# phi_q times KV in a linear-attention kernel: from whole-array matmuls to pairs on two 64-row halves

## The chip, the cores and the metric

The kernel runs on one core of one Trainium2 chip. Its time is the device time of one launch in microseconds (us). The kernel before takes 290.5 us, the median of 4 runs (290.08 to 291.49). A core has a matrix engine (PE, with weight loads shown as PEld), a vector engine (DVE), a scalar engine (ACT), a general engine (POOL), and SP, whose queue issues most DMAs here. PE multiplies a stationary operand, loaded first, with a moving one that streams past it column by column; results go to PSUM, from where DVE or ACT copy them to SBUF. An operand's row in the array is its partition, and both may occupy only a part of the 128 rows.

## The reference

The input x has 2048 rows of 640 features, in bfloat16. One pre-norm transformer block is computed, with linear attention of 32 heads of 20 features, and a gated feed-forward part of width 1536:

```python
qkv = layernorm(x) @ wqkv                       # q, k, v: 32 heads of 20
pq, pk = q @ w_phi, k @ w_phi                   # per head
phi_q = concat(softmax(pq), softmax(-pq))       # 40 features a head
phi_k = concat(softmax(pk), softmax(-pk))
kv, z = phi_k.T @ v, sum(phi_k)                 # per head, over all rows
o = (phi_q @ kv) / (phi_q @ z + 1e-6)
h = x + o @ wo
out = h + (gelu(layernorm(h) @ w_gate) * (layernorm(h) @ w_up)) @ w_down
```

## The kernel before

The 2048 rows are cut into 16 tiles of 128, and four tiles make a block. Matmuls and SP's DMAs run in the order in which the code is written out by hand; a function `weave` puts the steps of the attention of later tiles between the units (`gate_up`, `down`) of the feed-forward part of a block. All engines keep the order of the code, so one that waits holds what stands behind it.

*First stage.* For each tile, x is normalised and transposed. `fold` (L188) multiplies the weights of k, and later those of q, with w_phi, so that the exponent's argument comes out of one product; ACT and DVE in turn copy the result out of PSUM (L208, L210). `k_tile` computes it for k, and ACT makes `E`, exp of plus and of minus the argument. `k_norm` divides on the v side: DVE sums each head's exponentials, and `vt` is v with a column of ones, scaled by the reciprocal, by POOL or DVE (L269). `kv_tile` (L274) accumulates E.T @ vt over all tiles in one PSUM tile `kvp`. It does so for 64 features at a time, in two column halves of the array: features of the first half of a 128-feature chunk go to partitions 0 to 63 of the output, the others to 64 to 127, and each piece takes the four heads that its 64 features can touch, 4 x 21 = 84 columns. There are 20 such matmuls for a tile, two signs by five chunks by two halves.

*KV.* `kv_mask` (L285) writes the heads' own blocks from `kvp` into `KV`, which has 128 features by 5 chunks by 2 signs by 8 heads by 22 columns (20 of v, one of sums, and one of ones, put there beforehand from a mask `hmask`, L354 to L356, by POOL). It takes four instructions on DVE for one sign and four on POOL for the other, because the position of the four heads among the eight of a chunk differs by chunk and half. Products with features of another head are zeroed by the mask.

*Queries.* `q_mm` and `q_exp` make `Eq`, exp of plus and minus the argument of q, features on partitions, in chunks of 128. `attn_a` (L393) multiplies it with KV for one tile of rows: the stationary operand is 128 features of `Eq` by 128 rows, the moving one is the part of `KV` of the heads concerned. The result for all heads and signs, `AB`, has 2 x 32 x 22 columns. They are made in three groups of 11, 11 and 10 heads, the first two in one PSUM tile of two banks, the third in another. A chunk of 128 features touches 7 or 8 heads and may lie in two groups, so there are 14 matmuls for a tile, of 44 to 176 columns:

```python
pieces = [(s, c, max(h0, H0[c]), min(h1, H0[c] + NH[c])) for s in range(2) for c in range(NC)]
pieces = [x for x in pieces if x[2] < x[3]]
```

The first PSUM tile is copied to SBUF by ACT (L412), the second by ACT, and for tiles 0 and 1 by DVE (L415). Steps `attn_b` to `attn_b3` form the denominators (`pr`, `den`, `rd`, `w`) and the output `o` on POOL and DVE; then `o` is transposed, multiplied with wo (`attn_c`, L464), and added to x; the second layernorm follows, and `gate_up` (L504) and `down` (L519).

PSUM tiles of the second half of the program come from a ring of four (`psG2`), each of two banks, in the order of the code: a new tile waits until the one four places earlier has been copied out.

Of the kernel before, what the change touches and what calls it, by code (L numbers as in the profile page):

```python
# [8 lines left out]
BF16 = mybir.dt.bfloat16  # L9
F32 = mybir.dt.float32  # L10
ALU = mybir.AluOpType
# [6 lines left out]
def kernel(  # L18
# [12 lines left out]
    nc = tc.nc  # L31
    P = 128
    S = 2048
    D = 640
    H = 32
    Dh = 20
# [3 lines left out]
    NC = D // P  # L40
    NF = FF // P
    EPS = 1e-5
    HD = D // 2

    H0 = [(P * c) // Dh for c in range(NC)]
    NH = [(P * c + P - 1) // Dh - H0[c] + 1 for c in range(NC)]
# [2 lines left out]
    QT = (15, 15, 15, 15)  # L49
    VC = Dh + 1  # L50
    KC = Dh + 2
    UH = 11
    NU = 3

    G0 = [64 * j // Dh for j in range(2 * NC)]

    x_v = A_x.rearrange("b (p t) d -> p (b t) d", t=NT)
    o_v = out.rearrange("b (p t) d -> p (b t) d", t=NT)
# [3 lines left out]
    const = ctx.enter_context(tc.tile_pool(name="const", bufs=1))  # L62
# [9 lines left out]
    Wo = const.tile([P, NC, D], BF16, name="Wo")  # L72
    Wg = const.tile([P, NC, FF], BF16, name="Wg")
    Wu = const.tile([P, NC, FF], BF16, name="Wu")
    KV = const.tile([P, NC, 2, 8, KC], BF16, name="KV")

    Eq = [const.tile([P, 2, 2, 512], BF16, name=f"Eq{j}") for j in range(NB * NC // 2)]
    ident = const.tile([P, P], BF16, name="ident")
    hmask = const.tile([P, NC, 8], BF16, name="hmask")
    BD = const.tile([P, NC, 8, Dh], BF16, name="BD")  # L80
    nhalf = const.tile([P, 2], F32, name="nhalf")

    def eq(t, c, s):
        j = t // 4 * NC + c
        return Eq[j // 2][:, j % 2, s, t % 4 * P:(t % 4 + 1) * P]
# [4 lines left out]
    def gtile(name):  # L90
        return psG.tile([P, 2, 512], F32, name=name, tag="G")
# [45 lines left out]
    Wq2 = mid.tile([P, NC, D], BF16, name="Wq2")  # L137
# [3 lines left out]
    Wk2 = p1.tile([P, NC, D], BF16, name="Wk2")  # L141
# [5 lines left out]
    WkT = fp.tile([P, NC, D], BF16, name="WkT")  # L147
    WqT = p1.tile([P, NC, D], BF16, name="WqT")
# [25 lines left out]
    for c in range(NC):  # L174
        off = P * c - Dh * H0[c]
        nc.gpsimd.affine_select(out=hmask[:, c, :], in_=hmask[:, c, :], pattern=[[-Dh, 8]],
                                compare_op=ALU.is_ge, fill=0.0, base=off, channel_multiplier=1)
        nc.gpsimd.affine_select(out=hmask[:, c, :], in_=hmask[:, c, :], pattern=[[Dh, 8]],
                                compare_op=ALU.is_ge, fill=0.0, base=Dh - 1 - off, channel_multiplier=-1)
# [5 lines left out]

    warm(NWARM)

    def fold(WT, W2):  # L188


        runs = []
        for c in range(NC):
            lo, hi = H0[c] * Dh, (H0[c] + NH[c]) * Dh
            for u in range(2):
                a, b = max(lo, u * HD), min(hi, (u + 1) * HD)
                if a < b:
                    runs.append((u, c, a, b))
        runs.sort()
        for d in range(NC):
            wa = gtile("wa")  # L200
            for i, (u, c, a, b) in enumerate(runs):
                nc.tensor.matmul(wa[:, u, a - u * HD:b - u * HD], lhsT=WT[:, c, d * P:(d + 1) * P],
                                 rhs=BD[:, c].rearrange("p a b -> p (a b)")[:, a - H0[c] * Dh:b - H0[c] * Dh],
                                 start=(i == 0 or runs[i - 1][0] != u),
                                 stop=(i + 1 == len(runs) or runs[i + 1][0] != u), skip_group_check=True)
            dst = W2[:, d, :].rearrange("p (u f) -> p u f", u=2)
            if d % 2 == 0:
                nc.scalar.copy(dst, wa[:, :, 0:HD])  # L208
            else:
                nc.vector.tensor_copy(dst, wa[:, :, 0:HD])  # L210

    lnp, Ek, Vt = {}, {}, {}

    def ln_st(*tiles, act=True):
        for t, v in zip(tiles, ln_stats(p1, [x_sb[t // 4][:, t % 4, :] for t in tiles], "1", act)):
            lnp[t] = v
# [8 lines left out]
    def ln_tp(t):  # L225
        transpose_to(LN1T[t // 4][:, :, t % 4 * P:(t % 4 + 1) * P], lnp[t], True)
# [22 lines left out]
    def v_tile(t):  # L249
        v_mm(t)  # L250
        v_ev(t)

    def k_tile(t):
        pk = gtile("pk")
        proj(pk, t, Wk2)
        Ek[t] = ev.tile([P, 2, D], BF16, name="E", bufs=8)
        for s in range(2):
            nc.scalar.activation(Ek[t][:, s, :].rearrange("p (u f) -> p u f", u=2), pk[:, :, 0:HD],  # L258
                                 ACTF.Exp, scale=(1.0 if s == 0 else -1.0))
# [12 lines left out]
    kvp = psK.tile([P, 2, 512], F32, name="kvp")  # L272

    def kv_tile(t):  # L274

        for s in range(2):
            for c in range(NC):
                for u in range(2):
                    g0 = G0[2 * c + u]
                    nc.tensor.matmul(kvp[u * 64:(u + 1) * 64, s, c * 4 * VC:(c + 1) * 4 * VC],  # L280
                                     lhsT=Ek[t][:, s, c * P + u * 64:c * P + (u + 1) * 64],
                                     rhs=Vt[t][:, s, g0:g0 + 4, :],
                                     start=(c == 0 and t == 0), stop=(t == NT - 1), skip_group_check=True)

    def kv_mask():  # L285

        kp = kvp[:, :, 0:NC * 4 * VC].rearrange("p s (h f) -> p s h f", f=VC)

        nc.vector.tensor_scalar_add(kp[:, :, :, Dh], kp[:, :, :, Dh], 0.5e-6)
        nc.scalar.copy(acc.rearrange("p c h f -> p (c h f)"), kvp[:, 0, 0:NC * 4 * VC])  # L290
        for s, eng, src in ((1, nc.vector, kvp[:, 1, 0:NC * 4 * VC].rearrange("p (c h f) -> p c h f", h=4, f=VC)),
                            (0, nc.gpsimd, acc)):
            for u, c0, c1 in ((0, 0, 5), (1, 0, 2), (1, 2, 3), (1, 3, 5)):
                h = G0[2 * c0 + u] - H0[c0]
                r = slice(u * 64, (u + 1) * 64)
                eng.tensor_tensor(KV[r, c0:c1, s, h:h + 4, s:s + VC], src[r, c0:c1],
                                  hmask[r, c0:c1, h:h + 4, None].to_broadcast([64, c1 - c0, 4, VC]), ALU.mult)

    pqs = {}

# [10 lines left out]
    def q_exp(j, signs=(0, 1)):  # L311
        for s in signs:
# [19 lines left out]

    nc.vector.tensor_tensor(BD, wphi[:, :, None, :].to_broadcast([P, NC, 8, Dh]),
                            hmask[:, :, :, None].to_broadcast([P, NC, 8, Dh]), ALU.mult)
# [1 line left out]
    v_tile(2)  # L336
    ln_ap(3, on_pe=True)
    ln_st(4, 5, act=False)
    fold(WkT, Wk2)
    ln_tp(3)  # L340
    fp_cm.__exit__(None, None, None)
    ev_cm = tc.tile_pool(name="ev", bufs=1, side="right", reuse_waits="tile")
# [2 lines left out]
    for t in range(NT):  # L345
        k_tile(t)
        if t == 0:
            ln_ap(4, on_pe=True)
            ln_tp(4)
            ln_ap(5, on_pe=True)  # L350
            ln_st(6, 7)
        if t == 1:
            ln_tp(5)
            nc.gpsimd.memset(KV, 0.0)  # L354
            nc.gpsimd.tensor_copy(KV[:, :, 0, :, KC - 1], hmask)
            nc.gpsimd.tensor_copy(KV[:, :, 1, :, 0], hmask)  # L356
        if t == 12:
            fold(WqT, Wq2)
        if t + 3 < NT:
            v_tile(t + 3)  # L360
        if 6 <= t + 5 < NT:
            ln_ap(t + 5, on_act=True)
        if t % 2 == 1 and t + 7 < NT:
            ln_st(t + 7, t + 8)
        k_norm(t)
        if t % 2 == 1 and t >= 5:
            kv_tile(t - 5)
            kv_tile(t - 4)
        if t == 10:
            nc.sync.dma_start(Wo, wo_v)  # L370
            nc.sync.dma_start(Wu, wu_v)
        for j in range(len(QT)):
            if t == QT[j]:
                q_mm(j)
                q_exp(j)
    q = len(QT)
    for t in range(12, NT):
        kv_tile(t)
# [14 lines left out]
    def attn_a(t, dve=False):  # L393

        b = t // 4
        if b not in LN2T:
            LN2T[b] = p2.tile([P, NC, 512], BF16, name="LN2T", bufs=2)
        AB = p2r.tile([P, 2, H, KC], F32, name="AB", bufs=2)
        for v in range(2):
            ab = gtile("ab")  # L400
            for i in range(2 - v):
                h0 = UH * (2 * v + i)
                h1 = min(h0 + UH, H)
                pieces = [(s, c, max(h0, H0[c]), min(h1, H0[c] + NH[c])) for s in range(2) for c in range(NC)]
                pieces = [x for x in pieces if x[2] < x[3]]
                for j, (s, c, ha, hb) in enumerate(pieces):
                    nc.tensor.matmul(  # L407
                        ab[:, i, s * UH * KC + (ha - h0) * KC:s * UH * KC + (hb - h0) * KC],
                        lhsT=eq(t, c, s), rhs=KV[:, c, s, ha - H0[c]:hb - H0[c], :],
                        start=(j == 0), stop=(j == len(pieces) - 1), skip_group_check=True)  # L410
            if v == 0:
                nc.scalar.copy(AB[:, :, 0:2 * UH, :].rearrange("p s (u h) f -> p u s (h f)", u=2),  # L412
                               ab[:, :, 0:2 * UH * KC].rearrange("p u (s f) -> p u s f", s=2))
            else:
                (nc.vector.tensor_copy if dve else nc.scalar.copy)(  # L415
                    AB[:, :, 2 * UH:H, :].rearrange("p s h f -> p s (h f)"),
                    ab[:, 0, 0:2 * UH * KC].rearrange("p (s f) -> p s f", s=2)[:, :, 0:(H - 2 * UH) * KC])
        st[t] = AB

    def attn_b(t, on_pe=False):  # L420
# [222 lines left out]
```

The softmax here doesn't subtract the row's maximum and nothing guards it: scores larger than these inputs give would overflow.

## Time and profile before

The profile is of one execution, and shows what each engine did and waited for.

| | us |
|---|---|
| median of the runs | 290.5 |
| the profiled execution | 290.86 |
| its span, first to last instruction | 289.2 |
| copy of the first part of AB, ACT, L412 | 0.963 each, 16 times |
| copy of the second part of AB, ACT, L415 | 0.536 each, 14 times |
| copy of the second part of AB, DVE, L415 | 0.612 each, twice |

A row of instructions gives the line, engine, operation, tiles written and read, the shape, and busy time with the mean of one in nanoseconds. For matmuls the end, and so the duration, is modelled, and successive matmuls overlap; the distance between starts is what they cost. Three stages matter: up to about 79 us k, v and KV are made; from 79.4 to 103.1 the queries and the attention of the first tiles; then the feed-forward part, with the attention of later tiles between.

### The profile page before, as it was taken

How to read it: one execution, taken by the hardware profiler on the slowest of the kernel's cores; microseconds unless marked ns; L12 is line 12 of the kernel's file. 1: busy time of each engine (PE TensorE's matmuls, PEld its weight loads, DVE VectorE, ACT ScalarE, POOL GpSimd, SP SyncE). 2: the span in 40 equal slices, each digit the busy share in tenths (PEclk: the TensorE clock that was granted, in tenths of full speed). 3: DMA queues.
4: the chain of work that ended last, by engine and by line, in shares of the span. 5: the costliest groups of instructions: out<-in, count | busy, mean ns of one | idle time of the engine just before them, and what ended most of it. 6: DMA issues, size and time to landing. Idle time of an engine off the chain costs nothing.

```text
span 289.2 us, 5553 instructions
## 1 busy us (share of the span) xinstructions
PE 275.7 (95%) x2218; PEld 177.4 (61%) x2233; DVE 167.7 (58%) x287; ACT 144.1 (50%) x228; POOL 98.8 (34%) x207
## 2 busy tenths in 40 slices
PE   7798899989999899999999999999999999999995
PEld 2475577765555688778875555576555567444473
DVE  6689999988367466675623656532484832323322
ACT  2379778765968866536425445331445441123200
POOL 6228977866320223643421136220124340000000
PEclk9999999999999999999999999999999999999999
DMA  7997413290080011425310112222011322000011
GB/s 207 226 329 242 64 32 70 48 354 32 2 272 2 0 22 27 56 59 71 68 45 25 25 23 46 49 54 82 2 31 21 64 45 83 33 1 0 2 45 45
DMA packets 40970, 21.03 MB, mean 73 GB/s; under 512 B 33136, under 2 KB 39280, under 8 KB 40944
## 3 DMA queue, kind: packets, MB, share of 16 engines
q1 hardware_dynamic: 39856, 19.67, 27.9%
q10 hardware_dynamic: 1088, 1.01, 1.1%
q8 instruction: 17, 0.28, 0.4%
q14 instruction: 9, 0.07, 0.1%
HBM read 10.18 MB, written 2.62 MB: 44 GB/s over the span
## 4 chain that ended last, share of the span: by engine, by line
PE 81%; DVE 6%; DMA 5%; ACT 4%; issue 2%; POOL 1%; SPq 0%; ACTq 0%; DVEq 0%; POOLq 0%
PE gu L504 33%; PE pd L519 18%; PE pq L308 7%; PE po L464 7%; PE pv L235 5%; PE pk L235 5%; PE ab L407 3%; DMA Wv<-in_A_wqkv_dram 3%; DVE sk L264 2%; PE kvp L280 2%; DMA oT<-o 1%; DMA LN1T<-ln 1%; ACT Eq L313 1%; DVE vt L269 1%; ACT E L258 1%
## 5 line engine op out<-in xcount | busy, mean ns | idle before, releaser
L507 ACT ACTIVATE g<-gu 128x512 bf16<-128x512 f32 (+1 forms) x60 | 30.7, 512 | 74.9 <-PE gu L504 69.8
L510 DVE TENSOR_TENSOR GT<-gu,g 128x512 bf16<-128x512 f32 (+1 forms) x60 | 34.5, 581 | 56.7 <-ACT g L507 56.5
L504 PE MATMUL gu<-LN2T,Wg 128*128 128x512 bf16 (+1 forms) x293 | 61.4, 335 | 1.6 <-DVE LN2T L130 0.6
L504 PE MATMUL gu<-LN2T,Wu 128*128 128x512 bf16 (+1 forms) x296 | 61.2, 336 | 0.1
L519 PE MATMUL pd<-Wd,GT 128*128 128x320 bf16 x384 | 53.9, 299 | 0.0
L519 PEld LDWEIGHTS <-GT 128*128 128x128 bf16 x384 | 37.5, 98 | 15.6 <-DVE GT L510 0.9
L504 PEld LDWEIGHTS <-Wu 128*128 128x128 bf16 x300 | 29.3, 98 | 22.6
L504 PEld LDWEIGHTS <-Wg 128*128 128x128 bf16 x300 | 29.0, 98 | 21.3 <-issue 1.5
L235 PEld LDWEIGHTS <-LN1T 128*128 128x128 bf16 x320 | 30.5, 98 | 16.9 <-DMA LN1T<-ln 2.8
L269 POOL TENSOR_TENSOR vt<-vS,rs 128x672 bf16<-128x672 bf16 x22 | 34.5, 1588 | 8.9 <-DVE rs L266 7.3
L525 DVE TENSOR_TENSOR y<-pd,x_sb 128x640 bf16<-128x640 f32 (+1 forms) x17 | 13.3, 784 | 30.7 <-PE pd L519 30.7
L235 PE MATMUL pv<-Wv,LN1T 128*128 128x320 bf16 x160 | 24.2, 299 | 4.0 <-DMA LN1T<-ln 2.2
L464 PE MATMUL po<-Wo,oT 128*128 128x320 bf16 x160 | 24.4, 299 | 0.4 <-DMA oT<-o 0.4
L235 PE MATMUL pk<-Wk,LN1T 128*128 128x320 bf16 x160 | 24.2, 299 | 0.3 <-DVE Wk L210 0.3
L445 DVE TENSOR_TENSOR tt<-AB,w 128x1280 bf16<-128x1280 f32 x16 | 23.8, 1486 | 1.2 <-POOL w L438 0.9
L258 ACT ACTIVATE E<-pk 128x640 bf16<-128x640 f32 x32 | 20.7, 702 | 7.0 <-PE pk L235 6.9
L264 DVE TENSOR_REDUCE sk<-E 128x64 f32<-128x1280 bf16 x16 | 23.2, 1450 | 0.8 <-ACT E L258 0.8
L308 PE MATMUL pq<-LN1T,Wq 128*128 128x512 bf16 x96 | 22.7, 379 | 0.6 <-ACT Eq L313 0.4
L412 ACT COPY AB<-ab 128x968 f32<-128x968 f32 x16 | 15.4, 963 | 14.7 <-PE ab L407 14.5
L313 ACT ACTIVATE Eq<-pq 128x1024 bf16<-128x1024 f32 x20 | 19.4, 1025 | 3.4 <-PE pq L308 3.4
L464 PEld LDWEIGHTS <-oT 128*128 128x128 bf16 x160 | 15.5, 98 | 8.0 <-DMA oT<-o 1.2
L487 POOL TENSOR_SCALAR v<-sm 128x1 f32<-128x1 f32 x14 | 8.4, 599 | 31.4 <-DVE x_sb L478 31.4
(75 smaller groups left out, 277.2 us busy)
## 6 DMA issues: line engine op xcount, KB each, us to landing
out_dram<-y SPq DMA_DIRECT2D x15, 160.0 KB, 1.8
Wg<-in_B_w_gate_dram SPq DMA_DIRECT2D x1, 1920.0 KB, 11.3
Wu<-in_B_w_up_dram SPq DMA_DIRECT2D x1, 1920.0 KB, 9.3
Wd<-in_B_w_down_dram SPq DMA_DIRECT2D x1, 1920.0 KB, 7.8
x_sb<-in_A_x_dram SPq DMA_DIRECT2D x2, 640.0 KB, 5.7
Wv<-in_A_wqkv_dram SPq DMA_DIRECT2D x2, 400.0 KB, 8.4
Wo<-in_A_wo_dram SPq DMA_DIRECT2D x1, 800.0 KB, 4.9
x_sb<-in_A_x_dram ACTq DMA_DIRECT2D x1, 640.0 KB, 8.6
```

The source lines that it names most:

```text
L235: nc.tensor.matmul(ps[:, u, 0:HD], lhsT=lnT(t, c), rhs=W[:, c, u * HD:(u + 1) * HD], start=(c == 0), stop=(c == NC - 1))
L258: nc.scalar.activation(Ek[t][:, s, :].rearrange("p (u f) -> p u f", u=2), pk[:, :, 0:HD], ACTF.Exp, scale=(1.0 if s == 0 else -1.0))
L264: nc.vector.reduce_sum(sk, Ek[t].rearrange("p s (h f) -> p (s h) f", f=Dh), axis=AX.X)
L269: eng.tensor_tensor(vt[:, s], vS[t % 6], rs[:, s * H:(s + 1) * H, None].to_broadcast([P, H, VC]), ALU.mult)
L308: nc.tensor.matmul(pqs[j][:, i, :], lhsT=Wq2[:, kc, c * P:(c + 1) * P], rhs=LN1T[b][:, kc, :], start=(kc == 0), stop=(kc == NC - 1))
L313: nc.scalar.activation(Eq[j][:, :, s, :], pqs[j], ACTF.Exp, scale=(1.0, -1.0)[s])
L445: nc.vector.tensor_tensor(tt.rearrange("p s (h f) -> p s h f", f=Dh), num, w[:, :, :, None].to_broadcast([P, 2, H, Dh]), ALU.mult)
L464: nc.tensor.matmul(po[:, u, 0:HD], lhsT=st[t][:, c, :], rhs=Wo[:, c, u * HD:(u + 1) * HD], start=(c == 0), stop=(c == NC - 1))
L504: nc.tensor.matmul(gu[:, i, 0:n], lhsT=W[:, c, f * P:(f + 1) * P], rhs=LN2T[b][:, c, a0:a1], start=(c == 0), stop=(c == NC - 1))
L507: nc.scalar.activation(g[:, 0:n], gu[:, 0, 0:n], ACTF.Gelu_apprx_tanh)
L510: nc.vector.tensor_tensor(st[b, "g", f][:, a0:a1], gu[:, 1, 0:n], g[:, 0:n], ALU.mult)
L519: nc.tensor.matmul(pd[:, u, 0:HD], lhsT=st[b, "g", f][:, tl * P:(tl + 1) * P], rhs=Wd[:, f, u * HD:(u + 1) * HD], start=(f == 0), stop=(f ...
```

## The change

The features of q are put in another order. In each chunk of 128, the first 64 now belong to heads 0 to 15 and the other 64 to heads 16 to 31; `fold` writes the folded weights of q in that order. For k nothing is reordered, but `kv_tile` takes its 64 features from the first or the second half of the 640, so that the two halves of the partitions of `kvp` hold the same grouping. Every 64 features touch four heads, from head 3c of the half on, whatever the chunk c and the half. So KV has room for 4 heads instead of 8, one mask `kmask` serves all, and `kv_mask` takes one instruction on each engine.

`attn_a` uses 64 rows of the array at a time: a matmul has 64 features and 4 x 22 = 88 columns. Successive matmuls alternate between the upper and the lower rows and write different PSUM tiles, one for heads 0 to 15 and one for heads 16 to 31. There are 20 for a tile, and both PSUM tiles are taken before the first of them. Each is copied out whole, 2 x 352 columns.

```diff
-    KV = const.tile([P, NC, 2, 8, KC], BF16, name="KV")
+    KV = const.tile([P, NC, 2, 4, KC], BF16, name="KV")
...
+    UH = H // 2
+    HALF = (slice(0, 64), slice(64, P))
...
+    kmask = const.tile([P, NC, 4], BF16, name="kmask")
...
-            dst = W2[:, d, :].rearrange("p (u f) -> p u f", u=2)
+            dst, src = W2[:, d, :].rearrange("p (u f) -> p u f", u=2), wa[:, :, 0:HD]
+            if halves:
+                dst = W2[:, d, :].rearrange("p (c u f) -> p u c f", c=NC, u=2)
+                src = src.rearrange("p u (c f) -> p u c f", c=NC)
...
-                    g0 = G0[2 * c + u]
-                    nc.tensor.matmul(kvp[u * 64:(u + 1) * 64, s, c * 4 * VC:(c + 1) * 4 * VC],
-                                     lhsT=Ek[t][:, s, c * P + u * 64:c * P + (u + 1) * 64],
-                                     rhs=Vt[t][:, s, g0:g0 + 4, :],
+                    f0, h0 = u * HD + c * 64, u * UH + 3 * c
+                    nc.tensor.matmul(kvp[HALF[u], s, c * 4 * VC:(c + 1) * 4 * VC],
+                                     lhsT=Ek[t][:, s, f0:f0 + 64], rhs=Vt[t][:, s, h0:h0 + 4, :],
...
-            for u, c0, c1 in ((0, 0, 5), (1, 0, 2), (1, 2, 3), (1, 3, 5)):
-                h = G0[2 * c0 + u] - H0[c0]
-                r = slice(u * 64, (u + 1) * 64)
-                eng.tensor_tensor(KV[r, c0:c1, s, h:h + 4, s:s + VC], src[r, c0:c1],
-                                  hmask[r, c0:c1, h:h + 4, None].to_broadcast([64, c1 - c0, 4, VC]), ALU.mult)
+            eng.tensor_tensor(KV[:, :, s, :, s:s + VC], src, kmask[:, :, :, None].to_broadcast([P, NC, 4, VC]), ALU.mult)
...
-            nc.gpsimd.tensor_copy(KV[:, :, 0, :, KC - 1], hmask)
-            nc.gpsimd.tensor_copy(KV[:, :, 1, :, 0], hmask)
+            nc.gpsimd.memset(kmask, 1.0)
+            for r in HALF:
+                nc.gpsimd.affine_select(out=kmask[r], in_=kmask[r], pattern=[[4, NC], [-Dh, 4]],
+                                        compare_op=ALU.is_ge, fill=0.0, base=0, channel_multiplier=1)
+                nc.gpsimd.affine_select(out=kmask[r], in_=kmask[r], pattern=[[-4, NC], [Dh, 4]],
+                                        compare_op=ALU.is_ge, fill=0.0, base=Dh - 1, channel_multiplier=-1)
+            nc.gpsimd.tensor_copy(KV[:, :, 0, :, KC - 1], kmask)
+            nc.gpsimd.tensor_copy(KV[:, :, 1, :, 0], kmask)
...
-        for v in range(2):
-            ab = gtile("ab")
-            for i in range(2 - v):
-                h0 = UH * (2 * v + i)
-                h1 = min(h0 + UH, H)
...
-                    nc.tensor.matmul(
-                        ab[:, i, s * UH * KC + (ha - h0) * KC:s * UH * KC + (hb - h0) * KC],
-                        lhsT=eq(t, c, s), rhs=KV[:, c, s, ha - H0[c]:hb - H0[c], :],
-                        start=(j == 0), stop=(j == len(pieces) - 1), skip_group_check=True)
...
+        ab = gtile("ab"), gtile("ab")
+        for s in range(2):
+            for c in range(NC):
+                for u, r in enumerate(HALF):
+                    nc.tensor.matmul(ab[u][:, s, 3 * c * KC:(3 * c + 4) * KC], lhsT=eq(t, c, s)[r],
+                                     rhs=KV[r, c, s].rearrange("p h f -> p (h f)"),
+                                     start=(c == 0), stop=(c == NC - 1), skip_group_check=True)
+        for u in range(2):
+            (nc.vector.tensor_copy if dve and u == 1 else nc.scalar.copy)(
+                AB[:, :, u * UH:(u + 1) * UH].rearrange("p s h f -> p s (h f)"), ab[u][:, :, 0:UH * KC])
```

More of the change, by code (lines that the diff above doesn't have):

```diff
@@ L51 @@
     KC = Dh + 2
-    UH = 11
-    NU = 3
-    G0 = [64 * j // Dh for j in range(2 * NC)]
+    UH = H // 2
+    HALF = (slice(0, 64), slice(64, P))
     x_v = A_x.rearrange("b (p t) d -> p (b t) d", t=NT)
@@ L186, with fold @@
     warm(NWARM)
-    def fold(WT, W2):
+    def fold(WT, W2, halves):
         runs = []
@@ L205, in fold @@
                                  stop=(i + 1 == len(runs) or runs[i + 1][0] != u), skip_group_check=True)
-            dst = W2[:, d, :].rearrange("p (u f) -> p u f", u=2)
+            dst, src = W2[:, d, :].rearrange("p (u f) -> p u f", u=2), wa[:, :, 0:HD]
+            if halves:
+                dst = W2[:, d, :].rearrange("p (c u f) -> p u c f", c=NC, u=2)
+                src = src.rearrange("p u (c f) -> p u c f", c=NC)
             if d % 2 == 0:
-                nc.scalar.copy(dst, wa[:, :, 0:HD])
+                nc.scalar.copy(dst, src)
             else:
-                nc.vector.tensor_copy(dst, wa[:, :, 0:HD])
+                nc.vector.tensor_copy(dst, src)
     lnp, Ek, Vt = {}, {}, {}
@@ L338 @@
     ln_st(4, 5, act=False)
-    fold(WkT, Wk2)
+    fold(WkT, Wk2, False)
     ln_tp(3)
@@ L354 @@
             nc.gpsimd.memset(KV, 0.0)
-            nc.gpsimd.tensor_copy(KV[:, :, 0, :, KC - 1], hmask)
-            nc.gpsimd.tensor_copy(KV[:, :, 1, :, 0], hmask)
+            nc.gpsimd.memset(kmask, 1.0)
[6 more added lines that the diff above has]
+            nc.gpsimd.tensor_copy(KV[:, :, 1, :, 0], kmask)
         if t == 12:
-            fold(WqT, Wq2)
+            fold(WqT, Wq2, True)
         if t + 3 < NT:
@@ L398, in attn_a @@
         AB = p2r.tile([P, 2, H, KC], F32, name="AB", bufs=2)
-        for v in range(2):
-            ab = gtile("ab")
-            for i in range(2 - v):
-                h0 = UH * (2 * v + i)
-                h1 = min(h0 + UH, H)
[L404 to L407, printed above, removed]
-                        ab[:, i, s * UH * KC + (ha - h0) * KC:s * UH * KC + (hb - h0) * KC],
-                        lhsT=eq(t, c, s), rhs=KV[:, c, s, ha - H0[c]:hb - H0[c], :],
-                        start=(j == 0), stop=(j == len(pieces) - 1), skip_group_check=True)
[L411 to L417, printed above, removed]
+        ab = gtile("ab"), gtile("ab")
[8 more added lines that the diff above has]
+                AB[:, :, u * UH:(u + 1) * UH].rearrange("p s h f -> p s (h f)"), ab[u][:, :, 0:UH * KC])
         st[t] = AB
```

## The prediction

> **What bounds the kernel now.** The first section of the page and its clock row come first: is one engine the bound, and is it ever slowed?
>
> ```profile
> span 289.2 us, 5553 instructions
> PE 275.7 (95%) x2218; PEld 177.4 (61%) x2233; DVE 167.7 (58%) x287; ACT 144.1 (50%) x228; POOL 98.8 (34%) x207
> PEclk9999999999999999999999999999999999999999
> ```
>
> PE, the matmul engine, is busy for 95% of the span at its full clock, and no other engine reaches 60%. A busy PE need not be a limited one, so next the chain that ended last, summed by line:
>
> ```profile
> PE 81%; DVE 6%; DMA 5%; ACT 4%; issue 2%; POOL 1%; SPq 0%; ACTq 0%; DVEq 0%; POOLq 0%
> PE gu L504 33%; PE pd L519 18%; PE pq L308 7%; PE po L464 7%; PE pv L235 5%; PE pk L235 5%; PE ab L407 3%; DMA Wv<-in_A_wqkv_dram 3%; DVE sk L264 2%; PE kvp L280 2%; DMA oT<-o 1%; DMA LN1T<-ln 1%; ACT Eq L313 1%; DVE vt L269 1%; ACT E L258 1%
> ```
>
> The chain is PE's own instruction stream. The product that the change rewrites, `ab` on L407, holds 3% of it, so this is the most that can be won. The timeline of one call (tile 8), PE and its weight loads:
>
> ```profile
> 151.64 0.83 PEld L407 LDWEIGHTS <-Eq 128*128 128x128 bf16 x14
> 151.78 0.87 PE L407 MATMUL ab<-KV,Eq 128*128 128x154 bf16 x14
> 152.48 1.24 PE L504 MATMUL gu<-LN2T,Wg 128*128 128x512 bf16 x4
> ```
>
> The ends of matmuls are modelled, so I read starts: from 151.78 to 152.48 one call takes 0.70 us of PE, and 16 calls take 11.2. What follows begins at once. Last, the kernel already has one product on two halves of the array: `kvp` on L280, split by columns, in pairs. It is the nearest row to what comes:
>
> ```profile
> 35.23 1.53 PE L235 MATMUL pv<-Wv,LN1T 128*128 128x320 bf16 x10 [1.14 <-DMA LN1T<-ln]
> 36.70 0.95 PE L280 MATMUL kvp<-vt,E 128*64 128x84 bf16 x40
> 37.58 0.85 PE L235 MATMUL pk<-Wk,LN1T 128*128 128x320 bf16 x5
> ```
>
> **Price of a matmul.** Pieces of the chain give start to start: 10 of 512 columns in 2.16 us (216 ns), 10 of 320 in 1.36 (136), 5 of 128 in 0.28 (56). That is 0.417 ns a column plus 2.6 ns each. Check on `ab`: a call has 14 matmuls with 2 x 792 = 1584 columns: 660 + 36 = 696 ns, as measured. So columns, not weight loads, set its time.
>
> **Price of a pair and of the switch.** By this, 84 columns cost 37.6 ns. The ten `pv` that begin at 35.23 have streamed by 36.59, and `pk` begins at 37.58: 0.99 us for the 40 half-array matmuls. As 20 concurrent pairs they need 0.752; one after the other 1.50. They do run in pairs, and 0.235 us are left for entering and leaving. Single rows of the trace place it: 0.093 before the first `kvp`, 0.093 after the last, the rest on slower first pairs and the first full matmul afterwards. The two matmuls of a pair start 2 to 7 ns apart.
>
> **The product, changed.** A call becomes 20 matmuls of 64 rows and 88 columns (39.3 ns), as 10 pairs. The trace has no row-split matmul, so both ends. Low: pairs concurrent, no switch, 0.393 us. High: no overlap and a full switch, 0.786 + 0.235 = 1.02. I take the pair and the switch as `kvp` shows them: 0.393 + 0.235 = 0.63, a gain of 0.07 us a call, 16 x 0.07 = 1.2 us (1.1 to 1.3 by rounding). Most of what the pairing wins (0.31) goes to the switch, because a call is short: ten pairs and out again. Only a pair interval below (0.70 - 0.235) / 10 = 46.5 ns gains at all.
>
> Two rules of the Trainium skill speak against this. "TensorE: Matmul & The Clock Gate", section "Wait — 56ns, not 53.3ns?", gives about 25 ns below which matmul starts never come closer. By it a call is 20 x 25 + 235 = 735 ns, 0.035 over now: +0.6 us in all. The `kvp` row has 40 starts in 0.88 us, 22 ns each with the switch inside, so the floor doesn't hold across two halves, and I go by the row. The same page, section "LDWEIGHTS (loading the stationary operand)", says that a load's time depends on its columns and not on its rows. Then half-height loads are no cheaper, and they rise from 14 to 20 a call. The nearest row: where a 44-column matmul lies between loads of 128 columns, starts are 27 to 28 ns apart, though its columns need 21. If the loads of the two halves cannot overlap, a pair is at least 55 ns and a call 0.55 + 0.235 = 0.785, +1.4 us in all. `kvp` loads 64 columns, not 128, so it cannot exclude this; it stays as a rival.
>
> **What of the gain arrives.** After 103 us PE waits only three times for over 0.1 us (0.42 at 131.4, 0.20 at 142.8, 0.54 at 167.4), so nearly all of it does. Exceptions: from 97.7 to 103.1 the chain runs over ACT (exponentials, two `AB` copies, table load, gelu), and calls 2 and 3 lie beside it: 0.15 lost. I leave about 0.1 for the waits at 131.4 and 167.4, which end on other engines.
>
> **Copies out of PSUM.** Before, 968 elements (963 ns) and 440 (536) on ACT; after, twice 704, by these two points 750 each: 1.50 us as before. The first copy can no longer begin after 10 of 14 matmuls, since both tiles finish together; with the shorter call both are out within 0.1 us of before. For tiles 0 and 1 the second copy is on DVE: 440 elements take 612 ns, and 640 take 823 in the residual add, so 704 take about 890, +0.28. Behind it on DVE are `pr`, `den`, `rd`, `w`, `tt`, `o`, and PE's transpose waits for `o`; at tile 1 it has about 0.4 us to spare, of which two slower copies and an earlier PE take most: 0 to 0.2 lost, I take 0.1. ACT is 0.2 us freer per such tile.
>
> **Buffers.** Both `ab` tiles must now be free at the first matmul; before, the second had 0.48 us more. If PE waits there, the whole queue behind it (gate, up, down) does. Against the evictions of the trace the second had been free for over 0.14 us at each start except call 3 (100.8 us), where it waits 0.1 to 0.3 inside the stretch that ACT bounds. Nothing.
>
> **Edits at zero.** The mask of KV goes from four instructions to one on each engine: DVE 1.35 us to 0.59, POOL 2.16 to 0.89. PE meanwhile runs `pq` up to 81.68; only call 0, 0.75 long instead of 0.70, seems to have waited for POOL, 0.05. POOL's set-up at tile 1: a memset of half the size (1.56 to 0.8), a new memset (0.13), four masks at 0.2, two copies at 0.3: 2.3 us as before. Its cover is POOL's idle time in that stage; without it, 0.1. The regrouping of Wq is in the write of five existing copies, same element count: 0, at most 0.1 each where PE waits on two of them near 60 us. `kvp` keeps number and size of its matmuls. No DMA is added or moved.
>
> **Sum.** -1.2 + 0.15 + 0.1 + 0.1 - 0.05 = -0.9. The profiled execution, 290.86 us around its span of 289.2, would be 289.96; it lay 0.36 above the median of 290.5, and the median becomes 289.6.
>
> **The rivals.**
> - *Loads in turn* (0.17): pairs at 55 ns. For it: 27 ns for a full-width load. Against: halves have rows of their own. +1.4 gives 291.9, a little less if the first load hides in the switch.
> - *Halves in turn* (0.13), the slower side: row halves don't run together as column halves do, for example because both put out to all 128 partitions of PSUM. Place: each of the 160 pairs; price 39.3 ns a pair, 1.02 us a call, +0.32 x 16 = 5.1, 295.6. It decides from the 46.5 ns above. Against it: the two halves write separate banks here.
> - *No switch* (0.14): row halves need no drain, a call is 0.39, -0.31 x 16 = -4.9, of which calls 2 and 3 and DVE's copies keep back 0.9: 286.5. Against it: `kvp` pays it both ways, every time.
>
> **How the numbers follow.** Likeliest (0.55): 289.6, its own range 288.4 to 290.4, for a switch of 0.15 to 0.25 us; the residual 0.01 is anything else. A measurement tells 0.5% from no change, so faster means below 289.05 and slower above 291.95. Faster: 0.37 of the likeliest (0.20) and *no switch*, 0.34. Slower: *halves in turn*, two fifths of *loads in turn*, the residual, 0.21. The rest, 0.45, is the same. The range 286.2 to 292.0 takes in all but *halves in turn* and thin ends.
>
> **What the next profile would show.** Right: `ab` calls start to next start 0.60 to 0.65, pairs 39 ns apart and their halves under 10 ns, 0.09 us of nothing at each end. Starts 27 ns apart mean the loads; 39 apart one by one, the halves in turn; no gap at the ends, no switch. New waits of PE before L408 would break the buffer step; a PE wait over 0.2 us at the transpose of tile 1, the copy step. I am wrong above all if entering row halves costs something else than entering column halves.

## The result and the profile after

The changed kernel takes 289.83 us (median of 29 runs, 288.89 to 292.22) against 290.73 of the kernel before, measured beside it (48 runs): -0.90 us by the medians; the ratio of the runs is put at 0.9973, 95% interval 0.9959 to 0.9986. Forecast was -0.9. The profiled execution took 289.56 us around a span of 287.8, against 290.86 and 289.2.

The engines' shares barely move, from the page of the kernel after:

```profile
span 287.8 us, 5742 instructions
PE 273.9 (95%) x2314; PEld 171.8 (60%) x2329; DVE 167.9 (58%) x284; ACT 143.8 (50%) x228; POOL 98.0 (34%) x209
```

PE is still the bound. It has 96 matmuls and 96 loads more and is busy for 1.8 us less. The same call as in the prediction, tile 8, in the timeline of PE after:

```profile
151.01 0.98 PE L515 MATMUL pd<-Wd,GT 128*128 128x320 bf16 x6
151.92 0.57 PE L408 MATMUL ab<-KV,Eq 64*128 64x88 bf16 x20
152.42 1.04 PE L500 MATMUL gu<-LN2T,Wg 128*128 128x512 bf16 x3
```

Six `pd` at 136 ns from 151.01 have streamed by 151.83, and the next `gu` begins at 152.42: the call costs 0.59 us where it cost 0.70. In it are twenty matmuls, in pairs that run together, and two gaps, 151.83 to 151.92 and one of the same length at the end. Single rows give the starts within this call, in ns from its first:

```
0 3 | 39 42 | 87 90 | 126 129 | 165 168 | 204 207 | 243 247 | 282 286 | 322 325 | 361 364 | next work 498
```

The halves start 3 ns apart and pairs 39, with one step of 48 after the second pair. Sixteen calls, 0.11 each, are 1.8 us. The first whole-array matmul behind a call costs 10 ns more than those after it, so that PE saves 1.6. Not all of that arrives, and PE's waits show where, before and after (us in total, times, longest):

```profile
PE tp L129 <- DVE ln L121: 0.7, 2, 0.4
PE gu L504 <- DVE GT L510: 0.5, 2, 0.3
PE po L464 <- DMA oT<-o: 0.4, 1, 0.4
```

```profile
PE tp L130 <- DVE ln L122: 0.9, 2, 0.6
PE gu L500 <- DVE GT L506: 0.8, 2, 0.5
PE po L460 <- DVE GT L506: 0.5, 1, 0.5
```

The first two waits have grown: PE is earlier and the other engines are not. The `po` rows are two different places. That of before is at 167.4 us and is gone after. That of after is at 142.8 us, where PE needs the transposed `o` and waited 0.20 us before the change. What ended this wait is named differently from trace to trace; by the time of landing it is the DMA of `oT`, as shown further below.

### The profile page after: what moved, and what is told of

Its sections match the earlier page's. It is cut to its first block, busy times and chain, and to the rows that moved or that the text cites. A ratio compares the mean times of both kernels' runs of the same rounds, so it can differ in the third digit from the quotient of the medians.

```text
span 287.8 us, 5742 instructions
## 1 busy us (share of the span) xinstructions
PE 273.9 (95%) x2314; PEld 171.8 (60%) x2329; DVE 167.9 (58%) x284; ACT 143.8 (50%) x228; POOL 98.0 (34%) x209
## 4 chain that ended last, share of the span: by engine, by line
PE 73%; DVE 16%; ACT 3%; DMA 3%; issue 2%; POOL 2%; SPq 0%; DVEq 0%; ACTq 0%; POOLq 0%
PE gu L500 33%; PE pd L515 18%; PE pq L307 8%; PE po L460 7%; DVE sk L268 6%; DVE vt L273 3%; DMA Wv<-in_A_wqkv_dram 3%; DVE rs L270 2%; PE ab L408 2%; DVE stats L101 2%; PE pk L239 2%; PE pv L239 2%; ACT Eq L312 1%; PE kvp L284 1%; DVE mv L102 1%
## 5 line engine op out<-in xcount | busy, mean ns | idle before, releaser
L500 PEld LDWEIGHTS <-Wg 128*128 128x128 bf16 x300 | 28.4, 98 | 22.3 <-issue 1.7
L412 ACT COPY AB<-ab 128x704 f32<-128x704 f32 x30 | 21.0, 749 | 14.8 <-PE ab L408 14.5
```

What stands on the lines that cost most here:

```text
L412: (nc.vector.tensor_copy if dve and u == 1 else nc.scalar.copy)(AB[:, :, u * UH:(u + 1) * UH].rearrange("p s h f -> p s (h f)"), ab[u][:, ...
L500: nc.tensor.matmul(gu[:, i, 0:n], lhsT=W[:, c, f * P:(f + 1) * P], rhs=LN2T[b][:, c, a0:a1], start=(c == 0), stop=(c == NC - 1))
```

## Experiments

Three groups, each timed beside the kernel before. *The changed kernel again*, as the yardstick of the first and the third group:

> The changed kernel once more, as the yardstick for the others of its group and for what repeats in its trace. All theories: 0.9 us under the kernel before (0.4 to 1.2). A call of attn_a takes 0.60 us of PE from the end of the work before it to the next work. PE's waits at the transposed o near 143 us (0.7 us in the first trace) and near 167 us (none in the first trace, 0.54 in that of before) do not repeat if they are a matter of when a DMA happens to land, and repeat if the change causes them.

289.47 us against 290.59 (ratio 0.9969, 0.9945 to 0.9994). A call takes 0.594 us again. PE's wait near 142.7 repeats, at 0.40 to 0.74 us in three traces (0.20 before); that at 167 does not come back. In the trace of before, `oT` issued at 163.2 landed after 4.17 us; in those of after, 2.58. So 0.54 us of the 1.4 between the two spans is one DMA's landing. How many executions of the kernel before have it is not known, since one was profiled.

> The changed kernel as the yardstick of this group: about 0.9 us under the kernel before. PE waits 0.78 us at 98.6, 0.54 at 103.0, 0.62 at 131 and some tenths near 142.6 us, as in its first two traces.

290.25 against 290.72 (0.9986, 0.9964 to 1.0007), with the same waits, 0.78, 0.54, 0.63 and 0.74. (The first and third of these contain the 0.095 us of a gap.) This group alone doesn't tell the change from none. The gain is 0.90, 1.12 and 0.47 us in the three groups of runs, so differences of a few tenths between medians say little. The traces are steadier, and I use them below: the *stretch* from the first `pq` behind KV to the start of the last matmul leaves out the first stage, whose end scatters from 79.3 to 80.4 us.

**Do the halves run together because they alternate?**

```diff
-        for s in range(2):
-            for c in range(NC):
-                for u, r in enumerate(HALF):
+        for u, r in enumerate(HALF):
+            for s in range(2):
+                for c in range(NC):
```

> The order of the 20 matmuls of a call alone is changed: first the ten of the upper half, then the ten of the lower. Theory (the two halves run together only when neighbours in the queue use different halves): the ten pairs of 39 ns become 20 single matmuls of 39 ns, a call takes 0.59 + 0.20 = 0.98 us instead of 0.60, +0.39 x 16 = +6.2 us over the changed kernel, or +5 if calls 0 to 3 are absorbed where ACT sets the pace. Rival (the gain has nothing to do with the halves running together, but with fewer columns or the smaller mask): no change, within 0.5 us.

292.56, +3.1 over the changed kernel of its group: between the two. The timeline of its call at tile 8:

```profile
152.04 0.98 PE L515 MATMUL pd<-Wd,GT 128*128 128x320 bf16 x6
152.95 0.81 PE L408 MATMUL ab<-KV,Eq 64*128 64x88 bf16 x20
153.69 0.82 PE L500 MATMUL gu<-LN2T,Wg 128*128 128x512 bf16 x3
```

From 152.86 to 153.69 the call takes 0.84 us, not 0.98. The starts tell why:

```
0 38 86 125 164 203 243 | 251 282 289 321 337 359 376 | 415 454 493 533 572 611
```

After six steps of 39 to 48 ns, starts come in two interleaved series. A matmul cannot start 8 ns after one on the same rows when each needs 39; so the lower half's first has overtaken three of the upper half's that were still to start. The semaphores bear it out: the first matmul of the lower half is the one that waits for its own PSUM tile, and it is the eighth to start; the one that signals the end of the upper half is the thirteenth. In all 16 calls the eighth start comes 250 to 252 ns after the first, as if PE looked ahead over about four matmuls. My theory, "only neighbours", was too strict; that running together is what is won stands, since nothing else was changed and 0.25 us a call is lost. So an engine does not always keep the order of the code: here PE keeps it within each half of the rows, and not across the two.

**What does going in and out cost?**

```diff
+            if s == 0:
+                nc.tensor.matmul(ab[0][:, 0, 400:432], lhsT=ident, rhs=ident[:, 0:32],
+                                 start=True, stop=True, skip_group_check=True)
```

> Between the five pairs of one sign and the five of the other stands one matmul on the whole array, 32 columns, whose result nobody reads (16 ns by its columns). Theory (a change between whole array and halves costs 0.2 us for going in and out): a call takes 0.60 + 0.20 + 0.02 = 0.82 us, +3.5 us over the changed kernel, or +2.7 if calls 0 to 3 are absorbed. Rival (the gaps at the ends of a call are the first weight loads or an artefact of the trace, not a price of the change of mode): +0.3 us, for the matmul alone.

292.11, +2.6. One call:

```profile
151.81 0.98 PE L518 MATMUL pd<-Wd,GT 128*128 128x320 bf16 x6
152.72 0.37 PE L408 MATMUL ab<-KV,Eq 64*128 64x88 bf16 x10
153.02 0.19 PE L412 MATMUL ab<-ident 128*128 128x32 bf16 x1
153.15 0.37 PE L408 MATMUL ab<-KV,Eq 64*128 64x88 bf16 x10
153.45 0.82 PE L503 MATMUL gu<-LN2T,Wg 128*128 128x512 bf16 x3
```

0.82 us from 152.63 to 153.45, as forecast: one idle matmul of 32 columns in the middle costs 0.23, of which 0.21 are not its own columns. The gaps are the price of the change of mode.

**Is that price paid once per call?**

```diff
+        reps = 2
+        for i in range(reps):
+            for s in range(2):
+                for c in range(NC):
+                    for u, r in enumerate(HALF):
...
+                                         start=(c == 0 and i == 0), stop=(c == NC - 1 and i == reps - 1),
```

> Each call does its ten pairs twice in one go (numerator and denominator both double, so the output stays as it is, but for the small constant in the denominator). Theory: ten more pairs at 39 ns and no more switching, a call takes 0.99 us, +0.39 x 16 = +6.3 us over the changed kernel, or +5 if calls 0 to 3 are absorbed. Rival (the 0.20 us is spread over the pairs, by slow loads, not paid once per call): a call doubles to 1.2 us, +9.6 us.

295.41, +5.9.

```profile
153.67 0.98 PE L518 MATMUL pd<-Wd,GT 128*128 128x320 bf16 x6
154.58 0.96 PE L410 MATMUL ab<-KV,Eq 64*128 64x88 bf16 x40
155.47 0.82 PE L503 MATMUL gu<-LN2T,Wg 128*128 128x512 bf16 x3
```

A call of 40 takes 0.985 us, 0.39 more for ten pairs: paid once. Three calls give no time away, the waits behind calls 2, 3 and 7 shrink instead, which leaves 13 x 0.39 = 5.1. A wait of 1.46 us for `oT` at 111.4 comes on top, and the waits at 87.6 and 142.6 shrink by 0.19 and 0.21; the first of these, for `oT`, comes back in the next run.

**Which calls count?** The same repetition in four calls at a time (`2 if t < 4 else 1`, and `2 if 8 <= t < 12 else 1`).

> Calls 0 to 3 alone do their ten pairs twice, +0.39 us of PE each. Theory (PE waits for other engines behind calls 2 and 3, at 98.6 and 103.0 us, and the wait shrinks by what the call grows, so that these two calls' time, and with it their share of the gain, is worth nothing): only calls 0 and 1 count, +0.8 us over the changed kernel, about 290.4 where it takes 289.6. Rival (PE's time counts everywhere): +1.6 us.

> Calls 8 to 11 alone do their ten pairs twice. Both: PE is the bound in their stage, all four count, +1.6 us over the changed kernel, twice of what calls 0 to 3 cost. If it is no more than they cost, the theory of the absorbed calls falls.

This group had no run of the changed kernel, so the medians can only be set beside 289.94 of the four-part mask below and 289.5 to 290.2 of the changed kernel in the other groups. Calls 8 to 11: 291.12, +0.9 to +1.6 where +1.6 was forecast, which decides nothing. The stretch does: 206.74 us, beside 205.15 and 205.17 of the two traces of the changed kernel with the same wait at 142.7, +1.6. All four calls count. Calls 0 to 3: 291.54, +1.3 to +2.1, and by time the theory (+0.8) has missed and the rival's +1.6 is met. The trace shows otherwise: behind call 2 the wait falls from 0.78 to 0.39, behind call 3 from 0.54 to 0.13. From the first `pq` behind KV to the end of that wait it is 24.13 us instead of 23.55: +0.58, which is 0.78 for calls 0 and 1 less a wait of 0.19 at 87.5 that is gone. Calls 2 and 3 add nothing. Then PE stops for something else:

```profile
107.64 4.87 SPq L133 DMA_TRANSPOSE oT<-o  x2
111.86 1.40 PE L463 MATMUL po<-Wo,oT 128*128 128x320 bf16 x9 [1.47 <-DMA oT<-o]
```

The transpose issued at 107.64 landed after 4.17 us. In the twelve traces in which calls 2 and 3 are not doubled it took 2.57 to 2.63; in the one that doubles all, 4.39. The records of DMA packets show what came between. Besides the data, they have packets that bring instructions; from the pages of before and after:

```profile
q8 instruction: 17, 0.28, 0.4%
q8 instruction: 18, 0.29, 0.4%
```

A packet of this queue has 16 KB, takes 0.9 to 1.7 us, and comes after about every 250 instructions of PE; a second queue brings packets of 8 KB. In this run one of 16 KB began at 109.69 and ended at 110.61; the last packets of the transpose ran only behind it. With 80 matmuls and 80 loads more in calls 0 to 3 it comes here; in the changed kernel it comes at 113.8. This is so throughout: of the 392 transposes that the 14 traces have after 75 us, 62 landed later than 2.7 us, and each of these met a packet of instructions on its way; of the 330 others 40 did. No run was made to move such a packet on purpose.

**Is the smaller mask part of the gain?**

```diff
-            eng.tensor_tensor(KV[:, :, s, :, s:s + VC], src, kmask[:, :, :, None].to_broadcast([P, NC, 4, VC]), ALU.mult)
+            for u, c0, c1 in ((0, 0, 5), (1, 0, 2), (1, 2, 3), (1, 3, 5)):
+                r = HALF[u]
+                eng.tensor_tensor(KV[r, c0:c1, s, :, s:s + VC], src[r, c0:c1],
+                                  kmask[r, c0:c1, :, None].to_broadcast([64, c1 - c0, 4, VC]), ALU.mult)
```

> The mask of KV is again written by four instructions on DVE and four on POOL, as before the change. Theory (it lies beside PE's pq): DVE takes 1.35 us and POOL 2.16 instead of 0.60 and 0.90, the first call may wait up to 0.05 us, no change that can be measured (within 0.4 us of the changed kernel). Rival (the shorter mask is the gain): +0.8 us, all that was won.

289.94 (0.9975 of the kernel before, 0.9954 to 0.9996): the gain is still there, 0.67 us in this group. In its timeline:

```profile
79.83 2.15 POOL L298 TENSOR_TENSOR KV<-acc,kmask 64x420 bf16<-64x420 f32 x4 [4.38 <-ACT acc L293]
81.59 0.87 PE L411 MATMUL ab<-KV,Eq 64*128 64x88 bf16 x20
```

Call 0 takes 0.87 instead of 0.57 by the profile's measure. At the fifth pair it waits 0.28 us for POOL. That is what four instructions would cost the changed kernel. Of the gain over the kernel before, the mask is 0.04: there call 0 took 0.749 us where the next one took 0.704.

**What bounds a pair with few columns?** In each sign the first pair gets 352 columns, the four others 44.

> In each sign the first pair is widened to 352 columns and the other four pairs cut to 44 (two of their four heads, so two heads of every four are left out of the product and the output is not the reference's). Asked: what bounds a pair when its columns get few. By columns a pair of 44 takes 21 ns; if the loads of the two halves run together, but a load of 128 columns needs 27 to 28 ns as on the whole array, 27; if they take turns, 55. The 39 ns of the changed kernel exclude the last for 88 columns, so 21 or 27 are expected. Time: 16 x 2 x (149 + 4 x 27 - 5 x 39.3) ns = +1.9 us for 27, +1.2 for 21.

One run, 290.66 us. The pairs of 44 columns start 25 to 26 ns apart, where the columns alone need 21: nearer to the 27 of a full-width load than to the columns, and 12.6 ns for each matmul and load. Whether the loads set this, or a least distance of two starts on one half, the run doesn't separate. Its time, +0.4 to +1.2 over the changed kernel, can't tell 1.2 from 1.9.

**Can the lost part be had?** First, one copy is moved out of ACT's chain. `attn_a` with `late=True` copies the first PSUM tile by ACT and returns the copy of the second, on DVE, to be issued later:

```diff
-    attn_a(2)
+    second = attn_a(2, late=True)
     attn_e(1, True, True)
+    second()
```

> The changed kernel with one copy moved: the second PSUM tile of call 2 is copied by DVE, behind its copy of the transposed layernorm of tile 1, and not by ACT ahead of the load of gelu's table. Theory (the gain of calls 2 and 3 is lost in a chain over ACT: exponentials, two copies, table, gelu): the chain is 0.70 us shorter, the wait at 103.0 goes from 0.54 to about 0, -0.5 us against the changed kernel. Rival (that wait would end on DVE's copy of the transposed layernorm or on PE's own work anyway): no change.

289.46, -0.8 against the changed kernel of its group (ratio of the medians 0.9973; 0.9956 to 0.9992 when the runs are drawn again at random). The timeline, ACT's copy and table load and PE behind them:

```profile
99.87 0.75 ACT L412 COPY AB<-ab 128x704 f32<-128x704 f32 x1
100.02 0.88 DVE L412 COPY AB<-ab 128x704 f32<-128x704 f32 x1
100.64 1.28 ACT L508 ACT_TABLE_LOAD   x1
102.39 0.71 PE L505 MATMUL gu<-LN2T,Wu 128*128 128x256 bf16 x5
102.94 0.71 PE L505 MATMUL gu<-LN2T,Wg 128*128 128x256 bf16 x5
```

The table load stands behind one copy, and between the two `gu` rows, where PE waited 0.54 us, there are now the 0.55 of five matmuls and no more. These 0.54 us are what the trace gives the edit; the rest of the 0.8 is scatter of the medians.

Then, besides, two places in the weave:

```diff
-          attn_at(6, 13, SHORT))
+          attn_at(6, 13, (0, 2, 3, 5, 9, 9, 10, 12)))
-    weave(gus(0, 256, 512) + downs(0, (2, 3)), attn_at(7, 2, SHORT))
+    weave(gus(0, 256, 512) + downs(0, (2, 3)), attn_at(7, 2, (0, 1, 2, 3, 9, 9, 10, 12)))
```

> As the run with the late copy, and the divide-and-add step of tile 6 one unit later and the small steps of tile 7 one unit earlier in the weave. Theory: the wait at 131 us (0.62), behind DVE's tt and o of tile 6, goes, and the one near 142.6 (0.4) for tile 7's transposed o too: -1.4 us against the changed kernel, 288.3, or -0.9 if only one of the two goes. Rival (the waits only move to the next eviction behind tt): no better than the late copy alone.

288.94, the fastest here: 0.9936 of the kernel before (0.9912 to 0.9960), -1.3 us against the changed kernel of its group. In its trace the waits at 131 and 142.8 are gone, and a new one has come:

```profile
134.67 0.71 PE L505 MATMUL gu<-LN2T,Wu 128*128 128x256 bf16 x5
135.90 1.40 PE L465 MATMUL po<-Wo,oT 128*128 128x320 bf16 x9 [0.52 <-DMA oT<-o]
```

The output of tile 6, one unit later now, has to be transposed in time for its product, and is not.

> The three edits of order of the run before this one, made in the kernel before the change. Its waits there are 0.44, 0.42 and 0.20 us. Theory (what the change wins on PE, 0.11 us a call, is eaten in part by waits of PE for other engines, not by anything in the product itself): the kernel before gains less from the same edits, 0.5 to 0.9 us, and the distance between the two kernels with these edits is 1.2 to 1.7 us instead of 0.9. Rival (the change is worth 0.9 and no more): the distance stays 0.9.

290.60, -0.1 against the kernel before (0.9990, 0.9972 to 1.0007): less than I had expected, because a wait of 0.58 comes up in its trace at 135.9, and that at 167.4 stays (0.64; 0.54 before). With the same three edits the two kernels stand 1.66 us apart (0.9943; 0.992 to 0.996, drawn again as above). That this is near to the 1.6 that PE saves is in part luck: the wait of 0.64 at 167.4, for an `oT` that met a packet of instructions, is in this distance and has nothing to do with the product.

## Why the prediction was right, and where it was not

The total was met, 289.6 with its size of -0.9, and the mechanism too: the halves run together, a switch is paid both ways, and part of the gain is lost in waits. That the number was met so closely is luck in part: the product's gain was set too low, the waits too low as well, and late landings of DMAs, which the sum did not have, moved the total by up to half a microsecond either way.

- *Price of a pair*: right. 39.3 ns was forecast from the slope of whole-array matmuls, 39 measured; the halves overlap as column halves do. *Halves in turn* and *loads in turn* fall with it. Of the two rules that spoke against it, that of the starts does not hold across halves: 20 starts in 0.36 us are 18 ns each, below the 25 of the Trainium skill, "TensorE: Matmul & The Clock Gate", section "Wait — 56ns, not 53.3ns?". That of the loads agrees with the trace, 97 ns recorded for a load with 64 rows and with 128, but the loads of the two halves overlap and hide under the columns. With 44 columns a pair, not a matmul, stops at 25 to 26, so each half seems to have such a limit for itself.
- *Price of the switch*: the mechanism right, the size a little too high. 0.235 was taken from `kvp`, 0.21 measured: 0.095 at either end, 9 ns of one slower pair, and 10 ns on the first whole-array matmul afterwards. A call gains 0.10 and not 0.07; in all 1.6 and not 1.2. *No switch* falls.
- *What of the gain arrives*: too kind. Forecast lost: 0.15 in calls 2 and 3, and 0.1 at 131 and 167. Measured, without the switch's own gap: the wait at 98.6 grows from 0.57 to 0.68, at 103.0 from 0.44 to 0.54, at 131 from 0.42 to 0.54, which is the whole of calls 2, 3 and 7 (0.33).
- *Copies*: ACT 749 ns and DVE 888 for 704 elements, 750 and 890 forecast. PE waits 0.19 us at 87.5, where 0.1 was taken, but not at the place that was feared. The transposes (`tp`) start on time; the `pq` behind them waits for DVE alone, by its semaphore, and starts 0.05 us after the end of DVE's longer copy (87.46): what it lacked was a PSUM tile. With it, calls 0 and 1 lose what they had won: up to the end of the wait at 103.0 the stretch is 23.59 us before and 23.55 in all three traces after.

```profile
86.57 0.88 DVE L412 COPY AB<-ab 128x704 f32<-128x704 f32 x1
87.04 0.44 PE L130 MATMUL tp<-ident,o 128*128 128x128 bf16 x5
87.51 2.32 PE L307 MATMUL pq<-LN1T,Wq 128*128 128x512 bf16 x10
```

- *Buffers*: right where it looked. Before every call PE shows only the 0.095 to 0.107 of the switch, at call 3 too. It did not look at the products that take over the tiles of `ab` afterwards.
- *Edits at zero*: right. The writes of Wq last as long as before (694 and 792 ns), POOL's set-up 2.4 us, and the shorter mask gives call 0 the 0.04 us for which 0.05 was forecast.
- *Not in the sum*: the landings of `oT`. Near 142.7 the wait grows from 0.20 to between 0.40 and 0.74. The transpose that it waits for was issued at 140.17 before and at 139.70 after, earlier by about as much as PE is, which alone would leave the wait as it was. But it took 2.58 us before and 2.79 to 3.12 in the three traces after, where a packet of instructions begins at 139.9 to 140.2. Before, that packet came at 147.4: the longer stream of PE's instructions brings it forward. At 167.4 the same works for the change: a packet at 165.2 made `oT` late before, and none comes there after.

The sum can be closed from the traces (us; calls with the 10 ns behind them; waits without the gaps of the switch):

| stretch | calls | waits of PE for engines | waits for `oT` | all |
|---|---|---|---|---|
| before | 11.29 | 2.22 | 0.75 | 206.27 |
| after | 9.66 | 2.72 | 0.75 | 205.15 |
| after, again | 9.66 | 2.72 | 0.45 | 204.84 |
| after, third | 9.66 | 2.73 | 0.77 | 205.17 |
| upper half first | 13.62 | 1.75 | 0.44 | 207.83 |
| whole-array matmul between | 13.32 | 1.81 | 0.20 | 207.34 |
| all calls twice | 15.93 | 1.30 | 1.66 | 210.93 |
| calls 0 to 3 twice | 11.23 | 1.70 | 1.82 | 206.79 |
| calls 8 to 11 twice | 11.23 | 2.73 | 0.76 | 206.74 |

What is left in each row, 192.0 us, is the same within 0.03. So the change is -1.63 in the calls, +0.50 in waits for engines where +0.3 was forecast, and 0 to -0.3 in landings: -1.1, -1.1 and -1.4 in the three traces, beside the -0.9 of the medians. The rows below show it from the other side: where all calls grow, by 3.7 to 6.3 us together, the waits for engines shrink by 0.9 to 1.4.

## What to carry to other kernels

Splitting the rows pays when enough pairs stand between going in and coming out: here 10 pairs of 88 columns save 0.31 us and the two changes of mode take 0.21 back. Count the mode changes as you count matmuls. And before you book what PE saves, look at the waits behind it: a saving ahead of a wait for another engine lengthens that wait by the same amount, and moving one copy out of the way took 0.54 us of such a wait away, about half of what the whole change brings. And a longer stream of instructions moves the packets that bring it: look whether a DMA that something waits for now meets one.

## What the runs showed of the hardware that I had not expected

- PE lets matmuls of one half of the rows overtake those of the other: in the order with ten upper ones first, the lower half starts, 251 ns after the first, while about four of the upper are unfinished.
- Changing between the whole array and halves leaves a gap of 0.093 to 0.097 us each way, for column halves (`kvp`) and row halves (`ab`) alike; `ab` behind `pd` at tile 6 shows 0.107. The first whole-array matmul afterwards takes 10 to 11 ns more from start to start, behind both kinds of halves.
- Transposing DMAs of one and the same shape land after 2.57 us in most cases, and in 1 to 6 cases of the 28 of each execution after 3 to 4.9, not always the same ones. All 62 that took over 2.7 us met a packet of instructions; none of the 290 that met no such packet did.
